# The last 64 queries of a short pair: scores of two heads in one full-size product

## The chip, the cores and the metric

The program runs on one core of one Trainium2 chip. The metric is the device time of one execution, in microseconds. Times of the kernel before: 1029.75 us median of three runs (1027.41 to 1031.17).

## The reference

One attention layer with a compressive memory, then two dense feed-forward layers. Inputs have batch 4, 8 heads, 576 positions, head size 64.

```
scores = q k^T / 8, causal;  a = softmax(scores);  local = a v
q_p = elu(q) + 1
mem = (q_p M) / (q_p z + 1e-6)            # per head, M is 64x64, z is 64
x = g * mem + (1 - g) * local             # g = sigmoid(beta), one per head
x = [2304 tokens, 512]
x = gelu-like(x w_in) w_out               # h * sigmoid(1.702 h), 512 -> 2048 -> 512
x = hswish(x w2_in) w2_out                # h * clip(h + 3, 0, 6) / 6
```

## The kernel before

The tokens are cut in six tiles of 384. A batch's first 384 queries are a tile of their own (a long segment, g = 0); its last 192 queries (a short segment, g = 1) share a tile with those of another batch. Heads go in pairs: a tile with a long segment has 4 pairs, one with two short segments has 8. Tiles 2 and 5 hold the short segments, 16 short pairs in all.

The feed-forward layers run as a stream of units (layer, tile, f), f over 16 blocks of 128 hidden features. A unit computes h (four quarters of 128 inputs, each three f32r products: L393, L395, L396), the gate (ScalarE L329, VectorE L332, ScalarE L341, GpSimd L344), and then y of the unit before (L364 to L366). h has one PSUM bank, so the next h waits until VectorE's L332 has read the last one. Tile 0 of layer 0 uses exact f32 products (L391, L362), which the trace shows as two records each.

The attention of the next tile runs beside the current tile's units, in steps that `pump` (L1023) emits between quarters. So the short pairs run beside tiles 1 and 4 of layer 0. `PG1` (L30) is the share of a tile's 128 steps over which the attention of a tile of short pairs is spread. A scheduler puts the instructions of each engine in order from modelled times; inside an engine they run strictly in that order. `chains` are generators that are stepped on as the emission goes; `need` runs one to its end.

For a short pair the steps are: `scores` (L612), which computes s for the first 128 queries of both heads (two banks), and then s4 and s5, the products of the last 64 queries of both heads with 512 and 64 keys. Head a lies in partitions 64a to 64a + 63 of q and k, so each is a product of a 64x64 piece that writes partitions 64a to 64a + 63 of the bank (L677 to L680). `soft4` (L682) takes their minimum on VectorE (L684, L685), the exponentials on ScalarE (L687, L688), the inverse on VectorE, and scales them on GpSimd (`norm`, L548). The 512-column part is turned through memory: `over` (L576) copies it as 16-bit words on ScalarE (L584) and issues a transposing DMA on SyncE (L590), and `join` (L593) copies the turned words into `pt` on VectorE (L609). The 64-column part, the diagonal block (tile `p5`, 128x64), is transposed on TensorE in `turn` (L726, bank `t4b`), and its copy goes to `t4` (L709). `mem_read` (L799) computes the memory term in bank `mem`, which VectorE scales into `mo` (L818 to L822). `weigh` (L834) sums everything in bank `o`: transposes of `mo`, products of `pt` with v, and of `t4` with v; ScalarE copies it to x (L886).

The banks of s, s4, s5, t4b, mem and o are taken from a ring of three (`bank`, L431). A run of products in a bank waits for the last reader of that bank. The loop that interleaves the pairs is at L953; the line that sets the order of a pair is L965.

Of the kernel before, what the change touches and what calls it, by code (L numbers as in the profile page):

```python
# [8 lines left out]
F32 = mybir.dt.float32  # L9
# [13 lines left out]
N0, N1 = 384, 192  # L23
# [3 lines left out]
CR = 8.5  # L27
OFF = 3
PG0 = (0.85, 0.8)
PG1 = 0.78  # L30
TB = 3
PB = 6
RB = 3
# [24 lines left out]
CROSS = 8  # L58
# [11 lines left out]


STEP = 768.0
ROUND = 352
BIG = 3.4028234e38
MZ = 132
TILES = [
# [37 lines left out]
def attention_moe_kernel(ctx: ExitStack, tc: tile.TileContext, qk0, sk0, sk1, vm0, vm1, bb, w1, w2, out):  # L114
# [305 lines left out]
    pairs = []  # L420
# [36 lines left out]
    def at_matmul(out, **args):  # L457
        on_pe[:] = [PE.matmul(out, **args).ins]  # L458
# [29 lines left out]
    def at_transpose(*args):  # L488
        on_pe[:] = [PE.transpose(*args).ins]

    def attention(ap, room, across):
# [4 lines left out]

        t4 = ap.tile([128, 2, 64], F32, tag="t4", bufs=1, name="t4")
        POOL.memset(t4, 0.0)

        def start(key, gen):  # L500
            gens[key] = chains.start(after_gates(gen, AB))
# [7 lines left out]
        def load_qk(i):  # L509

            if i >= NPAIR:
                return
            ti, si, b, g, p, _ = pairs[i]
            t = room[0].tile([128, 2 * N0], F32, tag="raw", bufs=RB if i < CROSS else RB2, name="qk")
            if g == 0:
                move(1, out=t, in_=qk0[b, p])
                qk[i] = (t[:, 0:N0], t[:, N0:2 * N0])
            else:
                for a in range(2):
                    h = slice(64 * a, 64 * a + 64)  # L520
                    move(3, out=t[h], in_=sk1[b, 2 * p + a][h])
                qk[i] = (t[:, 0:N1], t[:, N1:N1 + S])

        def load_vm(i):
            if not 0 <= i < NPAIR:
# [86 lines left out]
        def scores(i):  # L612

            ti, si, b, g, p, _ = pairs[i]
            norms[1] = ti
            q, k = qk[i]
            st = ap.tile([128, 12], F32, tag="st", name="st")
            mx, su = st[:, 0:6], st[:, 6:12]

            def product(banks, blocks):  # L620

                mm = in_a_run(free(banks[0]) + free(banks[1]))
                for o0, o1, c0 in blocks:
                    for a in range(2):
                        h = slice(64 * a, 64 * a + 64)
                        mm(
                            banks[a][:, o0:o1], lhsT=q[h, c0:c0 + 128], rhs=k[h, 0:o1 - o0], start=True, stop=True
                        )

            def soft(s, cols, dst, c):  # L630

                jobs = [(a, c0, c1, c + a * len(cols) + x) for a in range(2) for x, (c0, c1) in enumerate(cols)]
                yield
                for a, c0, c1, k in jobs:
                    masked_min(s[a][:, c0:c1], mask[:, 512 - (c1 - c0):512], BIG, mx[:, k:k + 1])
                yield
                for a, c0, c1, k in jobs:
                    d = expo(dst[a][:, c0:c1], s[a][:, c0:c1], mx[:, k:k + 1], su[:, k:k + 1])
                    if c1 == cols[-1][1]:
                        has_read(s[a], d)  # L640
                yield
                inverse(su[:, c:c + len(jobs)])
                yield
                for a, c0, c1, k in jobs:
                    norm(dst[a][:, c0:c1], su[:, k:k + 1], omg[:, 2 * p + a:2 * p + a + 1])
                if i >= CROSS:
                    yield
                    for a in range(2):
                        yield from over(i, a, dst[a], *merges0[g][c > 0])

            pp[i] = []
            if g == 0:
                parts = (((0, 128, 0), (128, 384, 128)), ((0, 384, 256),))
            else:
                parts = (((0, 512, 0),),)
            def weights(a):
                return room[0].tile([128, 512], F32, tag="p", bufs=PB2 if i >= CROSS else PB, name="p")

            t = [[None if i >= CROSS else weights(a) for _ in parts] for a in range(2)]
            pp[i] = [tuple(x) for x in t]  # L660
            c = 0
            for x, blocks in enumerate(parts):
                s = [bank("s") for _ in range(2)]
                if i >= CROSS:
                    for a in range(2):
                        t[a][x] = weights(a)
                product(s, blocks)
                start(("s", i, x), soft(s, [(o0, o1) for o0, o1, _ in blocks], [t[a][x] for a in range(2)], c))
                c += 2 * len(blocks)
                yield  # L670
            if g == 1:
                t = room[0].tile([128, 512], F32, tag="p", bufs=PB2 if i >= CROSS else PB, name="p4")
                t2 = ap.tile([128, 64], F32, tag="p5", name="p5")
                pp[i].append((t, t2))
                s, s2 = bank("s4"), bank("s5")
                mm = in_a_run(free(s) + free(s2))
                for o, c0, c1 in ((s, 0, 512), (s2[:, 0:64], 512, 576)):  # L677
                    for a in range(2):
                        h = slice(64 * a, 64 * a + 64)
                        mm(o[h], lhsT=q[h, 128:N1], rhs=k[h, c0:c1], start=True, stop=True)  # L680

                def soft4(s=s, s2=s2, t=t, t2=t2):  # L682
                    yield
                    masked_min(s, mask[:, 0:1].to_broadcast([128, 512]), BIG, mx[:, 2:3])  # L684
                    masked_min(s2[:, 0:64], mask4, mx[:, 2:3], mx[:, 3:4])  # L685
                    yield
                    has_read(s, expo(t, s, mx[:, 3:4], su[:, 2:3]))  # L687
                    has_read(s2, expo(t2, s2[:, 0:64], mx[:, 3:4], su[:, 3:4]))  # L688
                    yield
                    DVE.tensor_tensor(out=su[:, 2:3], in0=su[:, 2:3], in1=su[:, 3:4], op=ALU.add)  # L690
                    inverse(su[:, 2:3])
                    yield
                    norm(t, su[:, 2:3], omp[:, p:p + 1])
                    norm(t2, su[:, 2:3], omp[:, p:p + 1])
                    if i >= CROSS:
                        yield
                        yield from over(i, None, t, 512, [(0, 4, None)])

                start(("s", i, 2), soft4())
                yield  # L700

        def evac(i, jobs):
# [11 lines left out]
        def turn(i):  # L714
            ti, si, b, g, p, _ = pairs[i]
            if i >= CROSS:
                need(("s", i, 0), ("s", i, 1), ("s", i, 2))
                for k in (0, 1, None):
                    if k is not None:
                        head(i)  # L720
                    for n, (a, blocks, turned) in enumerate(joins[i]):
                        if a == k:
                            start(("j", i, n), join(i, a, blocks, turned))
                    if k == 1 and g == 1:
                        ps2 = bank("t4b")
                        at_transpose(ps2[0:64, 0:128], pp[i][2][1], ident)  # L726
                        start(
                            ("t", i, 0, 1),
                            evac(i, [(DVE, t4[0:64], ps2[0:64, 0:128].rearrange("p (a c) -> p a c", a=2), ps2)]),
                        )  # L730
                    yield
                if g == 0:
                    yield
# [65 lines left out]
        def mem_read(i):  # L799
# [7 lines left out]
            nb = len(rr)  # L807
            for k, r0 in enumerate(rr):
                at_matmul(a[:, k * 130:(k + 1) * 130], lhsT=e[:, r0:r0 + 128], rhs=m, start=True, stop=True)
            o = ap.tile([128, NT], F32, tag="tmp", bufs=TB, name="mo")  # L810
            w = ap.tile([128, 3, 2], F32, tag="mw", name="mw")
            mo[i] = o
# [118 lines left out]
        yield from weigh(CROSS - 1)  # L931
        across(0)
        load_qk(CROSS)
        load_qk(CROSS + 1)
        need(("x", CROSS - 1))
        yield pairs[CROSS - 1][0]
# [14 lines left out]
            yield pairs[i][0]  # L951

        for i in range(CROSS, NPAIR):  # L953
            s = scores(i)
            if i == CROSS or pairs[i - 1][5]:
                yield from chunks(s, 1)
                yield from pause(2)
                yield from chunks(s, 9)
                begun(i)
            else:  # L960
                t, w = turn(i - 1), weigh(i - 1)
                yield from chunks(s, 1)
                yield from mem_read(i - 1)
                load_qk(i + 1)
                for gen, n in ((t, 1), (s, 1), (t, 1), (s, 9), (t, 9)):  # L965
                    yield from chunks(gen, n)
                begun(i)
                yield from chunks(w, 9)
            if pairs[i][5]:
                yield from pause(WAIT[pairs[i][3]])  # L970
                yield from mem_read(i)
                load_qk(i + 2)
                yield from ended(i, turn(i), weigh(i))
# [197 lines left out]
```

## Time and profile before

| what | value |
|---|---|
| median of three runs | 1029.75 us |
| the profiled execution's own time | 1029.37 us |
| its span, first to last instruction | 1027.6 us |
| TensorE busy | 996.6 us |
| ScalarE, VectorE, GpSimd busy | 552.3, 508.6, 304.5 us |
| mean granted TensorE clock | 0.993 |

The span is the time from the first to the last instruction; 1.8 us of the execution lie outside it. Rows of an engine's timeline give start and duration of an instruction, or of several alike (x8: eight records; the duration then reaches from the first start to the last end). Starts of products that follow each other tell their cost better than the durations, since products overlap. In brackets stands the idle time ahead of an instruction and what ended it.

### The profile page before, as it was taken

The page shows a single profiled execution, that of the slowest core. Times are in us where ns is not written, and L with a number is a line of the kernel's source. Part 1 is how long each engine was busy: PE and PEld are TensorE (multiplying, and loading weights), DVE is VectorE, ACT ScalarE, POOL GpSimd, SP SyncE. Part 2 cuts the span into 40 slices and gives each one's busy share as a digit, 9 for nine tenths or more (in the row PEclk, how much of TensorE's full clock was granted, in tenths as well). Part 3 has the DMA queues.
Part 4 walks back from the last instruction along what each step waited for, and adds up shares of the span by engine and source line. Part 5 has one row for each costly group of instructions (what it writes and reads, how often), then busy time and mean ns, then how long its engine had stood idle before and what let it go on. Part 6 is the DMA issues. An engine that isn't in the chain of part 4 may idle for free.

```text
span 1027.6 us, 15875 instructions
## 1 busy us (share of the span) xinstructions
PE 996.6 (97%) x5737; PEld 883.8 (86%) x5737; DVE 508.6 (49%) x1263; ACT 552.3 (54%) x1142; POOL 304.5 (30%) x346
## 2 busy tenths in 40 slices
PE   7899999888999999999989999999999999999998
PEld 4556557677888898888869999999999999999998
DVE  5887775677655447346554887951121211212110
ACT  5877766666665466366554987963232332323322
POOL 3512003433343334243322422232222222222221
PEclk8999999999999999999999999999999999999999
DMA  4844427675453044225543773010010000100000
GB/s 168 295 184 151 157 77 195 146 184 143 113 101 101 27 101 98 55 80 122 123 108 125 296 255 134 1 32 32 1 62 1 31 32 1 47 16 1 32 1 32
DMA packets 110175, 99.15 MB, mean 96 GB/s; under 512 B 80400, under 2 KB 89616, under 8 KB 110096
## 3 DMA queue, kind: packets, MB, share of 16 engines
q1 hardware_dynamic: 110096, 98.14, 32.9%
q8 instruction: 45, 0.74, 0.3%
q14 instruction: 34, 0.28, 0.1%
HBM read 61.41 MB, written 9.44 MB: 69 GB/s over the span
## 4 chain that ended last, share of the span: by engine, by line
PE 69%; DMA 4%; DVE 3%; ACT 3%; issue 2%; POOL 1%; SPq 0%; ACTq 0%; DVEq 0%; POOLq 0%
PE h L393 11%; PE y L364 10%; PE h L395 10%; PE h L396 10%; PE y L365 10%; PE y L366 10%; DMA xp<-sp 4%; PE o L474 3%; PE s L474 2%; ACT sp L584 1%; DVE pt L609 1%; PE mem L458 1%; ACT p L540 1%; POOL p L548 1%; DVE s L535 1%
## 5 line engine op out<-in xcount | busy, mean ns | idle before, releaser
L344 POOL TENSOR_TENSOR g<-t,g 128x384 fp32r<-128x384 f32 x173 | 185.3, 1072 | 467.1 <-ACT g L341 391.9
L393 PE MATMUL h<-xs,w 128*128 128x384 f32 x704 | 242.3, 344 | 9.8 <-DVE t L332 9.7
L395 PE MATMUL h<-xs,w 128*128 128x384 f32 x704 | 236.6, 336 | 0.0
L396 PE MATMUL h<-xs,w 128*128 128x384 f32 x704 | 236.6, 336 | 0.0
L365 PE MATMUL y<-g,w 128*128 128x384 f32 x704 | 236.0, 335 | 0.0
L364 PE MATMUL y<-g,w 128*128 128x384 f32 x704 | 235.4, 335 | 0.0
L366 PE MATMUL y<-g,w 128*128 128x384 f32 x704 | 219.0, 336 | 0.0
L336 DVE SCALAR_TENSOR_TENSOR t<-t,h 128x384 f32<-128x384 f32 x96 | 53.1, 553 | 277.5 <-ACT t L334 277.4
L548 POOL TENSOR_SCALAR p<-p,st,omg 128x128 f32<-128x128 f32 (+3 forms) x128 | 93.2, 740 | 212.5 <-DVE st L544 116.7
L393 PEld LDWEIGHTS h<-xs,w 128*128 128x128 f32 x704 | 132.6, 188 | 25.8 <-DVE t L332 12.5
L334 ACT ACTIVATE t<-h,three 128x384 f32<-128x384 f32 x96 | 56.2, 585 | 170.5 <-PE h L396 167.7
L341 ACT CAST g<-t 128x384 fp32r<-128x384 f32 x176 | 91.0, 517 | 95.7 <-DVE t L336 50.2
L395 PEld LDWEIGHTS h<-xs,w 128*128 128x128 f32 x704 | 132.7, 189 | 1.5 <-issue 1.5
L396 PEld LDWEIGHTS h<-xs,w 128*128 128x128 f32 x704 | 132.6, 188 | 0.9 <-issue 0.8
L365 PEld LDWEIGHTS y<-g,w 128*128 128x128 f32 x704 | 132.2, 188 | 0.9 <-issue 0.8
L364 PEld LDWEIGHTS y<-g,w 128*128 128x128 f32 x704 | 132.2, 188 | 0.4 <-issue 0.3
L366 PEld LDWEIGHTS y<-g,w 128*128 128x128 f32 x704 | 130.2, 188 | 1.7 <-POOL g L344 1.4
L540 ACT ACTIVATE p<-s,st 128x256 f32<-128x256 f32 (+4 forms) x160 | 82.2, 522 | 62.1 <-DVE st L535 59.3
L535 DVE CUSTOM_DVE_ANT_0 s<-s,mask 128x128 f32<-128x128 f32 (+3 forms) x144 | 72.4, 528 | 30.9 <-PE s L474 30.2
L584 ACT COPY sp<-p 128x1024 uint16<-128x1024 uint16 (+1 forms) x80 | 74.8, 957 | 23.6 <-POOL p L548 17.7
L609 DVE COPY pt<-xp 128x512 uint16<-128x512 uint16 (+3 forms) x112 | 63.5, 625 | 36.0 <-DMA xp<-sp 22.2
L332 DVE SCALAR_TENSOR_TENSOR t<-t,h 128x384 f32<-128x384 f32 x80 | 43.9, 550 | 54.3 <-ACT t L329 50.5
(79 smaller groups left out, 1111.1 us busy)
## 6 DMA issues: line engine op xcount, KB each, us to landing
r<-in_w_dram SPq DMA_DIRECT2D x64, 512.0 KB, 6.1
wt<-r SPq DMA_DIRECT2D x32, 256.0 KB, 2.4
vm<-in_vm_dram SPq DMA_DIRECT2D x16, 386.0 KB, 3.4
qk<-in_qk_dram SPq DMA_DIRECT2D x16, 384.0 KB, 3.4
qk<-in_sk_dram SPq DMA_DIRECT2D x32, 192.0 KB, 3.3
x2d<-yo SPq DMA_DIRECT2D x24, 192.0 KB, 1.9
xr<-x2d SPq DMA_DIRECT2D x24, 192.0 KB, 3.1
out_dram<-yo SPq DMA_DIRECT2D x24, 192.0 KB, 1.9
```

Of the source, the lines that this page charges most:

```text
L341: gated["ACT"].append(ACT.copy(out=g[:, 0], in_=t).ins)
L344: d = {"DVE": DVE, "POOL": POOL}[e].tensor_tensor(out=g[:, 1], in0=t, in1=f32(g[:, 0]), op=ALU.subtract)
L364: PE.matmul(ys[d], lhsT=w[:, 0, o:o + 128], rhs=g[:, 0], start=(f == 0), stop=False)
L365: PE.matmul(ys[d], lhsT=w[:, 1, o:o + 128], rhs=g[:, 0], start=False, stop=False)
L366: PE.matmul(ys[d], lhsT=w[:, 0, o:o + 128], rhs=g[:, 1], start=False, stop=(f == NF - 1))
L393: PE.matmul(h, lhsT=w[:, 0, c:c + 128], rhs=x[:, 0], start=first, stop=False)
L395: PE.matmul(h, lhsT=w[:, 1, c:c + 128], rhs=x[:, 0], start=False, stop=False)
L396: PE.matmul(h, lhsT=w[:, 0, c:c + 128], rhs=x[:, 1], start=False, stop=last)
L535: DVE.tensor_tensor_reduce(out=o, in0=o, in1=m, scale=-SCALE, scalar=init, op0=ALU.add, op1=ALU.min, accum_out=out)
L540: return ACT.activation(out=dst, in_=o, func=AF.Exp, scale=-1.0, bias=m, accum_out=s)
L548: (DVE, POOL)[e[norms[0] % len(e)]].tensor_scalar(out=dst, in0=dst, scalar1=s, scalar2=w, op0=ALU.mult, op1=ALU.mult)
L584: ACT.copy(out=halves[:, 0:2 * n].rearrange("p (h c) -> p h c", h=2), in_=src[:, 0:n].bitcast(U16).rearrange("p (c h) -> p h c", h=2),)
```

## The change

Both heads' last 64 queries are put in one 128x128 tile `bd`, with the queries of head 0 in its upper left block, those of head 1 in its lower right block, and zeros elsewhere. One product of `bd` with all 128 partitions of k gives the scores of both heads, head a in partitions 64a to 64a + 63 as before. `bd` is one tile that is filled with zeros once; two DMAs per pair load its blocks, for the next short pair, after the current pair's product is emitted (`load_bd`). The diagonal block `p5` becomes one 128x128 tile whose right half stays zero; it is transposed at full size, in `mem_read`, into the free columns 384 to 511 of bank `mem`, instead of in `turn` into a bank of its own. In the loop, the second step of `scores` of a short pair comes after two steps of `turn` instead of one. `PG1` goes from .78 to .9, and an unused table is made smaller (`ROUND`).

```diff
-PG1 = 0.78
+PG1 = 0.9
-ROUND = 352
+ROUND = 32
...
         POOL.memset(t4, 0.0)
+        bd = ap.tile([128, 128], F32, tag="bd", bufs=1, name="bd")
+        POOL.memset(bd, 0.0)
+        p5 = ap.tile([128, 128], F32, tag="p5", bufs=1, name="p5")
+        POOL.memset(p5, 0.0)
...
+        def load_bd(i):
+
+            short = [pair for pair in pairs[i:] if pair[3] == 1]
+            if not short:
+                return
+            ti, si, b, g, p, _ = short[0]
+            for a in range(2):
+                h = slice(64 * a, 64 * a + 64)
+                move(3, out=bd[h, h], in_=sk1[b, 2 * p + a][h, 128:N1])
...
-                t2 = ap.tile([128, 64], F32, tag="p5", name="p5")
+                t2 = p5[:, 0:64]
...
                 for o, c0, c1 in ((s, 0, 512), (s2[:, 0:64], 512, 576)):
-                    for a in range(2):
-                        h = slice(64 * a, 64 * a + 64)
-                        mm(o[h], lhsT=q[h, 128:N1], rhs=k[h, c0:c1], start=True, stop=True)
+                    mm(o, lhsT=bd, rhs=k[:, c0:c1], start=True, stop=True)
...
                 start(("s", i, 2), soft4())
+                load_bd(i + 1)
                 yield
...
-                    if k == 1 and g == 1:
-                        ps2 = bank("t4b")
-                        at_transpose(ps2[0:64, 0:128], pp[i][2][1], ident)
-                        start(
-                            ("t", i, 0, 1),
-                            evac(i, [(DVE, t4[0:64], ps2[0:64, 0:128].rearrange("p (a c) -> p a c", a=2), ps2)]),
-                        )
...
+            if i >= CROSS and g == 1:
+                need(("s", i, 2))
+                at_transpose(a[:, 384:512], p5, ident)
+                start(("t", i, 0, 1), evac(i, [(DVE, t4[0:64], a[0:64, 384:512].rearrange("p (a c) -> p a c", a=2))]))
...
         load_qk(CROSS)
+        load_bd(CROSS)
...
-                for gen, n in ((t, 1), (s, 1), (t, 1), (s, 9), (t, 9)):
+                for gen, n in ((t, 1), (s, 1), (t, 1), (s, 9), (t, 9)) if g == 0 else ((t, 1), (t, 1), (s, 9), (t, 9)):
```

The order on TensorE, in tile 1, where the third short pair's s4 follows the second pair's mem; first before, then the change (xs and w are operands of h, g and w those of y; `s_` with the larger number is s5).

```order
L458 MATMUL mem<-vm,phi 128x130 x2
L366 MATMUL y_1400<-g,w_1334 128x384
L366 MATMUL y_1401<-g,w_1334 128x384
L366 MATMUL y_1402<-g,w_1334 128x384
L366 MATMUL y_1403<-g,w_1334 128x384
L474 MATMUL s_1660<-qk 64x512 x2
L474 MATMUL s_1661<-qk 64x64 x2
L393 MATMUL h<-xs_1291,w_1555 128x384
```

```order
L458 MATMUL mem<-vm,phi 128x130 x2
L489 MATMUL mem<-ident,p_121 128x128
L364 MATMUL y_1409<-g,w_1340 128x384
L365 MATMUL y_1409<-g,w_1340 128x384
L366 MATMUL y_1409<-g,w_1340 128x384
L474 MATMUL s_1697<-qk,bd 128x512
L474 MATMUL s_1698<-qk,bd 128x64
L393 MATMUL h<-xs_1297,w_1549 128x384
```

The group of four products has become two, and the transposition of the diagonal block stands behind mem and ahead of the next s4; before it stood some twenty products behind that s4, ahead of o.

The order on VectorE, a little later in tile 1, around the copy of the third pair's turned s4 words (`pt<-xp` with 4x64); first before, then the change (`t<-t,h` is the gate that frees the bank of h, `mw` and `mo` scale mem, `t_117<-mem` copies the transposed diagonal block, w is weight work).

```order
L609 COPY pt<-xp 128x2x4x64 x2
L543 TENSOR_SCALAR st<-st 128x2
L544 RECIPROCAL st<-st 128x2
L332 SCALAR_TENSOR_TENSOR t<-t,h 128x384
L818 TENSOR_SCALAR mw<-mem 128x4
L819 RECIPROCAL mw<-mw 128x4
L820 TENSOR_TENSOR mw<-mw,gall 128x4
L275 TENSOR_TENSOR w_1947<-wt,w_1947 128x512
L822 TENSOR_TENSOR mo<-mem,mw 128x256
```

```order
L557 TENSOR_SCALAR st<-st 128x2
L558 RECIPROCAL st<-st 128x2
L332 SCALAR_TENSOR_TENSOR t<-t,h 128x384
L623 COPY pt<-xp 128x2x4x64 x2
L722 COPY t_117<-mem 64x128
L828 TENSOR_SCALAR mw<-mem 128x4
L829 RECIPROCAL mw<-mw 128x4
L275 TENSOR_TENSOR w_1905<-wt,w_1905 128x512
L830 TENSOR_TENSOR mw<-mw,gall 128x4
L832 TENSOR_TENSOR mo<-mem,mw 128x256
```

The gate and a reciprocal have moved ahead of the copy that waits for a DMA, and the copy of the diagonal block has come in behind it.

## Rows read from the trace of the kernel before

**Rows 1.** The page, part 1: busy us (share of the span), instructions, by engine
```profile
PE 996.6 (97%) x5737; PEld 883.8 (86%) x5737; DVE 508.6 (49%) x1263; ACT 552.3 (54%) x1142; POOL 304.5 (30%) x346
```
**Rows 2.** Windows of tiles 1 and 4: length, busy PE, PEld, DVE, ACT, POOL, clock
```profile
160.00:262.00 102.00, 91.91 (x579) 74.99 (x579) 71.91 (x196) 66.76 (x140) 39.96 (x41) 0.98 0.70 165
460.00:562.00 102.00, 97.18 (x635) 81.69 (x632) 57.20 (x181) 54.45 (x117) 31.77 (x40) 0.98 0.49 111
```
**Rows 3.** Waits of TensorE, 160 to 265 us: us in total, times, longest
```profile
PE h L393 <- DVE t L332: 5.4, 4, 2.0
PE o L474 <- DVE t L709: 1.8, 1, 1.8
PE t4b L489 <- DVE mo L822: 1.4, 1, 1.4
PE o L474 <- ACT p L540: 0.9, 1, 0.9
```
**Rows 4.** Waits of TensorE, 440 to 565 us
```profile
PE o L474 <- ACT p L540: 2.9, 1, 2.9
```
**Rows 5.** Timeline of TensorE around an s4 group: start, duration, instruction
```profile
541.24 0.34 PE L366 MATMUL y<-g,w 128*128 128x384 f32 x1
541.51 1.19 PE L474 MATMUL s<-qk 64*64 64x512 f32 x8
542.63 0.44 PE L393 MATMUL h<-xs,w 128*128 128x384 f32 x1
542.91 0.34 PE L395 MATMUL h<-xs,w 128*128 128x384 f32 x1
543.09 0.34 PE L396 MATMUL h<-xs,w 128*128 128x384 f32 x1
```
**Rows 6.** Exact f32 products of tile 0: group (busy, mean ns), then timeline
```profile
L391 PE MATMUL h<-x,r 128*128 128x384 f32 x128 | 44.8, 493 | 1.4 <-DVE g L332 1.2 <-ACT pt L707 0.2
...
139.50 2.85 PE L391 MATMUL h<-x,r 128*128 128x384 f32 x8 [0.31 <-DVE g L332]
```
**Rows 7.** Timeline of TensorE around mem and the next s4
```profile
194.29 0.61 PE L458 MATMUL mem<-vm,phi 128*128 128x130 f32 x4
...
194.91 0.33 PE L366 MATMUL y<-g,w 128*128 128x384 f32 x1
195.18 1.19 PE L474 MATMUL s<-qk 64*64 64x512 f32 x8
198.41 0.45 PE L393 MATMUL h<-xs,w 128*128 128x384 f32 x1 [2.04 <-DVE t L332]
```
**Rows 8.** Timeline of TensorE around a transposition of the diagonal block
```profile
185.49 0.27 PE L489 MATMUL t4b<-ident,p 128*64 128x128 f32 x1
185.52 0.42 PE L365 MATMUL y<-g,w 128*128 128x384 f32 x1
185.78 0.34 PE L366 MATMUL y<-g,w 128*128 128x384 f32 x1
```
**Rows 9.** Timeline of VectorE from one copy of turned s4 words to the next
```profile
196.84 0.79 DVE L609 COPY pt<-xp 128x512 uint16<-128x512 uint16 x2 [2.94 <-DMA xp<-sp]
...
197.80 0.55 DVE L332 SCALAR_TENSOR_TENSOR t<-t,h 128x384 f32<-128x384 f32 x1
...
200.40 0.69 DVE L535 CUSTOM_DVE_ANT_0 s<-s,mask 128x512 f32<-128x512 f32 x1
...
212.34 0.79 DVE L609 COPY pt<-xp 128x512 uint16<-128x512 uint16 x2 [2.64 <-DMA xp<-sp]
```
**Rows 10.** Timeline of GpSimd: scaling of both parts of an s4
```profile
220.97 3.13 POOL L548 TENSOR_SCALAR p<-p,st,omp 128x512 f32<-128x512 f32 x2
```
**Rows 11.** Timeline of TensorE: the s4 that this scaling belongs to
```profile
211.00 1.19 PE L474 MATMUL s<-qk 64*64 64x512 f32 x8
```
**Rows 12.** Timeline of SyncE: transposing DMAs of the pair of rows 7, two loads
```profile
200.92 2.66 SPq L590 DMA_TRANSPOSE xp<-sp  x2
203.74 1.14 SPq L156 DMA_DIRECT2D qk<-in_sk_dram  x2
```

More of the change, by code (lines that the diff above doesn't have):

```diff
@@ L953, in attention @@
         for i in range(CROSS, NPAIR):
+            g = pairs[i][3]
             s = scores(i)
```

## The prediction

> **What bounds the kernel now.** I read the busy shares first, then the waits of TensorE by stretch, then its timeline around the instructions that change. TensorE is busy 996.6 us, 97% of the span, and every other engine but its own weight loader at most 54% [rows 1], so a change counts only if it shortens TensorE's own stream or one of its stops. The changed work lies in two stretches in which the short pairs run beside a tile of layer 0: tile 1 (160 to 262 us) and tile 4 (460 to 562 us). There TensorE stands still for 102.0 - 91.9 = 10.1 and 102.0 - 97.2 = 4.8 us [rows 2]. The waits name what ended each stop [rows 3, 4]: a gate on VectorE that frees the bank of h, the exponentials on ScalarE that free the bank of the s4 product, and the copy of the transposed diagonal block.
>
> **The product (16 times).** Before, one group computes 512 and 64 columns for the two heads in 64x64 pieces, 8 records. One f32r product of 384 columns follows another after .18 us; the group starts .27 after its predecessor, takes 1.12 to the next start, and the product behind it needs .28 [rows 5]. So a group costs 1.12 + .09 + .10 = 1.31 us, and 16 cost 21.0. After, one product of the whole array does the same columns in 2 + 2 records. Exact full-size products of 384 columns are .337 us apart (eight take 2.85 and a single one .493, so (2.85 - .493) / 7 [rows 6]), .88 ns a column, so two records of 512 take .90. For the 64 columns the bounds are two records at .88 ns a column (.11) and two that take as long as the 130 columns of mem: four of those cost .62 - .18 = .44, .11 each [rows 7], so .22. I take .16. The same mem rows go from f32r to exact full-size products and back with no extra start time, so I add none. The new group costs 1.01 to 1.12, taken 1.06: .25 saved each, **4.0 us in all, bounds 3.0 to 4.8**.
>
> The Trainium skill, "TensorEngine Tiling (Array Packing)", Theoretical Speedup, gives up to 2x to a dimension of at most 64; read against this change, giving up the 64-row pieces would double the streaming and cost some 16 x 1.0 us. The rows speak otherwise here: the 8 records before need 1.12 us for two heads side by side, and one full-size product holds both heads at once, so it streams the columns once, as before. By the rule the time would be some 16 us longer, by the rows 4.0 shorter; I give the rule no chance of its own beyond the slow rival.
>
> **The transposition.** The 64-column one before costs .29 - .18 = .11 us between products [rows 8]; the full-size one streams 128 columns like a record of mem, .11 [rows 7]. I count 0, bounds -.3 and +.3 for 16. The Trainium skill, same page, Gotcha 2: Feature Incompatibilities, says that column tiling excludes the transpose mode for FP32; by it the full-size form should gain more than that, and the .11 before leaves it no room.
>
> **Stops that go.** A short pair took seven banks of three in turn: two s, mem, s4, s5, t4b, o. So o took the bank that s4 had just filled, and waited for its exponential, .9 us in tile 1 and 2.9 in tile 4 [rows 3, 4]; t4b took mem's and waited 1.4 for VectorE; and once o waited 1.8 for the copy out of t4b [rows 3]. With t4b inside mem's bank there are six: o takes mem's bank, which it needs emptied anyway, and the block is copied before the scaling of mem. These four stops, 7.0 us, lose their cause. What is late next is o's other inputs, the turned words of s4 and mem's scaled rows.
>
> **What holds part of it.** VectorE copies the turned words of a pair's s4 when their DMA lands, and what stands behind that copy waits with it. For the third pair the copy waited 2.94 us, and behind it the gate that frees h, which stopped TensorE for 2.04 [rows 7, 9]. In the changed order the gate stands ahead of the copy, so this stop and its like (rows 3: 5.4 us in four) move. But the minimum of the next s4 still stands behind the copy: 196.84 to 200.40, and from there to the next such copy 212.34, a cycle of 15.5 us [rows 9]. The gate leaves it (.55 [rows 9]); a reciprocal that leaves and the copy of the block that enters about cancel: some 15. TensorE's work per pair is the distance of two s4, 211.00 - 195.18 = 15.8, less the stop of 2.04: 13.8, after 13.5 [rows 7, 11]. So where the cycle rules, I take three pairs of tile 1, 15 - 13.5 = 1.5 us each stay as a stop, now in front of o: 4.5 us, and their .8 us of saved product time is swallowed too.
>
> **A wait that comes.** The transposition of the diagonal block now stands behind mem, ahead of the next s4. It needs the block scaled on GpSimd; all of TensorE's queue, the h and y products included, stands behind it. The longest case: s4 at 211.00, scaled at 220.97 + 3.13 = 224.10, 13.1 us later [rows 10, 11]; the third pair's s4 has its next mem some 12 us behind it by the changed order (36 to 40 f32r products at .18, one o, one s, one s4). I take 2.0 us in all for these waits, bounds 0 and 8.
>
> **Loads, fills, pace.** 32 loads of 64x64 enter SyncE's queue; one issue takes .57 us (1.14 for two [rows 12]), so 1.14 per pair. Each waits for the s4 that read the tile last, and the transposing DMAs of the next pair stand behind it; the fourth pair's came at 200.92, 5.7 us after its s4 at 195.18 [rows 7, 12], so the load hides in idle queue time. If each delay reached TensorE: 15 x 1.1 = 17 us, the far end. The two fills on GpSimd run before its first work: 0, at most the 3.1 us that two scalings took [rows 10]. The slower pace (.9 for .78) moves, in the order, only the last pair of a tile: its o now comes with little between it and the last quarter of the next tile's h. I charge .5 at each of two borders, 1.0 in all; bounds 0 and 2.0 each, the longest stop of an h.
>
> **The sum.** Tile 1: stops 10.1 before; after, 4.5 of the cycle, 2.0 of the block and some 1.0 of gates that nothing here touches, 7.5: -2.6. Tile 4, with no weight work on VectorE: 4.8 before, the 2.9 goes, some .3 comes: -2.6. Products -4.0, of which .8 is swallowed: -3.2. Borders +1.0. Together -7.4 us. The profiled execution took 1029.4 (span 1027.6), the median of the runs is 1029.75; 1029.4 - 7.4 gives **1022.0 us**, .8% under the median.
>
> **Rivals.** A: only the products get shorter, and every stop that goes comes back before o or s4, since the cycle through the DMA sets the pace in all pairs. For it: the 15.5 us cycle. Against: tile 4 has hardly a stop besides o's 2.9. Time: 1029.4 - 4.0 = 1025.4. B, slower: the early transposition blocks TensorE. It decides if the block is ready some 2 us later after its s4 than before, for VectorE and GpSimd work no less; then the 12 us of room are short in about half of 15 pairs by 1 us and in the like of the 13.1 case by 3, some 10 us with the stops of rows 3 and 4 kept: 1029.4 - 4.0 + 10 = 1035.4; at half that lateness 1030.4. For it: 13.1 in one pair of tile 1. Against: elsewhere in these stretches GpSimd idles for microseconds ahead of that scaling. C: the cycle was only a result of the stops, and nearly all 14.9 us of them shrink to 5: 1029.4 - 4.0 - 9.9 = 1015.5. That the block-diagonal tile isn't loaded in time, so that s4 waits for its DMA, is part of B: a load has the 13.5 us of a pair's work to land in.
>
> **Chances.** Forecast .55 (own range 1017 to 1024.6), A .26, B .11, C .08. The range that holds 8 in 10 is 1015 to 1030, from C's end to half of B. A measurement of this kernel tells about .5% from no change, so faster means under 1024.6: the forecast's .52, C's .08, and a little of A's, .05, .65 in all; slower means over 1034.9, or .07 of B and a bit of unknown, .08; the rest, .27, within.
>
> **What would show it.** The new s4 group should stand .18 behind its predecessor, last 1.0 to 1.1 us, and leave no longer second start behind it. The waits of o for an exponential and all of t4b should be gone. o should wait for the words' copy or mem's rows in tile 1, by 1 to 2 us in some pairs; the new transposition for GpSimd in one or two. I am wrong if the stops of the two stretches sum to over 13 us, if a DMA of the block-diagonal tile ends a wait of s4, or if full-size exact products of 512 columns come over .5 us a record.

## The result and the profile after

The changed kernel took 1016.74 us (median of four runs, 1014.47 to 1017.99) against 1030.46 of the kernel before on the same chip: ratio .9867, 95% interval .9836 to .9899. That is 13.7 us less, where 7.4 were forecast. It lies inside the range of 1015 to 1030 us, .3 below the forecast's own range (1017 to 1024.6), and nearest to rival C (1015.5), which had a chance of .08.

The head of the page of the changed kernel, to be read against [rows 1]:

```profile
span 1012.6 us, 15781 instructions
PE 988.6 (98%) x5673; PEld 884.6 (87%) x5673; DVE 513.0 (51%) x1263; ACT 551.4 (54%) x1142; POOL 307.4 (30%) x348
```

Its two stretches by windows (us, then busy time of TensorE, its loader, VectorE, ScalarE, GpSimd, then granted clock), against [rows 2]:

```profile
160.00:262.00 102.00, 94.81 (x587) 80.11 (x586) 76.72 (x204) 69.69 (x147) 41.70 (x43) 1.00 0.72 172
460.00:562.00 102.00, 101.39 (x644) 91.07 (x643) 67.81 (x184) 63.49 (x131) 37.71 (x40) 1.00 0.58 140
```

TensorE stands still for 7.2 us in tile 1 (10.1 before) and .6 in tile 4 (4.8 before). Its waits in the first stretch, against [rows 3] (total, times, longest):

```profile
PE s L474 <- ACT p L554: 2.2, 5, 0.8
PE h L393 <- DVE t L332: 2.0, 2, 1.1
PE o L474 <- DVE mo L832: 1.9, 1, 1.9
PE o L474 <- DVE pt L623: 0.8, 1, 0.8
PE mem L489 <- POOL p L562: 0.2, 1, 0.2
```

and in the second, against [rows 4]:

```profile
PE o L474 <- DVE mo L832: 0.6, 1, 0.6
```

No stop of o for an exponential is left, and t4b is gone. No stop is ended by a DMA of `bd`; those loads land 2.2 us after issue (median). The new group, against [rows 5] (start, duration):

```profile
477.12 0.33 PE L365 MATMUL y<-g,w 128*128 128x384 f32 x1
477.30 1.19 PE L474 MATMUL s<-qk,bd 128*128 128x512 f32 x4
478.29 0.42 PE L366 MATMUL y<-g,w 128*128 128x384 f32 x1
478.55 0.34 PE L364 MATMUL y<-g,w 128*128 128x384 f32 x1
```

It starts .18 behind its predecessor and takes .99 to the next start; the start after that comes .26 later, not the usual .18. So it costs .99 + .08 = 1.07 us, against 1.06 forecast and 1.31 before.

**Where the time went.** I split the span of each profiled run in three. Stops are the span less TensorE's busy time on the page. Clock is the sum of (1 - granted clock) x 4 us over windows of 4 us, up to 1000 us. The rest is busy time less that loss.

| | span | stops | clock | rest |
|---|---|---|---|---|
| before | 1027.6 | 31.0 | 6.8 | 989.8 |
| after | 1012.6 | 24.0 | 1.7 | 986.9 |
| difference | -15.0 | -7.0 | -5.1 | -2.9 |

The profiled runs differ by a little more than the medians. The changed kernel's was its fastest, with a mean granted clock of .998; the other three had .994 to .997, so part of the 5.1 us of clock belongs to this one run. Of these 5.1 us, 1.7 fall in the first 100 us, which the change hardly touches. The others stand behind two stops of the kernel before, one of 1.7 us in tile 1 (an h that starts at 213.89) and the one of 2.9 us that [rows 4] show. Around the latter:

```profile
526.00:532.00 6.00, 3.14 (x19) 1.91 (x17) 4.01 (x16) 3.46 (x7) 1.53 (x2) 0.98 0.26 60
532.00:538.00 6.00, 6.00 (x34) 3.98 (x35) 2.29 (x6) 1.91 (x5) 2.12 (x3) 0.74 0.35 95
```

After the stop the clock is .74 over 6 us, 1.6 us lost on top of the stop itself. The changed kernel has no such window between 100 and 1000 us.

### The profile page after: what moved, and what is told of

Read it like the earlier page. It is cut to its first block, busy times and chain, and to the rows that moved or that the text cites. A ratio compares the mean times of both kernels' runs of the same rounds, so it can differ in the third digit from the quotient of the medians.

```text
span 1012.6 us, 15781 instructions
## 1 busy us (share of the span) xinstructions
PE 988.6 (98%) x5673; PEld 884.6 (87%) x5673; DVE 513.0 (51%) x1263; ACT 551.4 (54%) x1142; POOL 307.4 (30%) x348
## 4 chain that ended last, share of the span: by engine, by line
PE 78%; DVE 7%; ACT 6%; DMA 5%; issue 3%; SPq 1%; POOL 1%; POOLq 0%; ACTq 0%; DVEq 0%
PE h L393 11%; PE y L366 11%; PE h L395 11%; PE h L396 11%; PE y L364 11%; PE y L365 11%; DMA xp<-sp 3%; PE o L474 3%; PE h L391 3%; PE y L362 3%; PE s L474 3%; ACT p L554 2%; DVE s L549 1%; ACT sp L598 1%; PE mem L458 1%
## 5 line engine op out<-in xcount | busy, mean ns | idle before, releaser
L623 DVE COPY pt<-xp 128x512 uint16<-128x512 uint16 (+3 forms) x112 | 68.6, 667 | 21.7 <-DMA xp<-sp 18.4
```

## The experiments

Each was timed in five rounds beside the kernel before, whose median was 1029.4 to 1029.8 us in the three sets. The forecast gave the gain to three things: the product, the shorter ring of banks, and the stops that go with it. The rivals were that it comes from the pace, and that the parts don't add.

**The parts, one at a time.** The kernel before with the product and its loads alone:

```
+                load_bd(i + 1)
...
-                    for a in range(2):
-                        h = slice(64 * a, 64 * a + 64)
-                        mm(o[h], lhsT=q[h, 128:N1], rhs=k[h, c0:c1], start=True, stop=True)
+                    mm(o, lhsT=bd, rhs=k[:, c0:c1], start=True, stop=True)
```

> The kernel before with the block-diagonal product and its loads alone; the transposition, its bank, the loop and the pace (.78) stay. My theory (products 4 us, the rest from stops of TensorE that go with the smaller ring of banks): 4 us faster than before, ratio .996, with the waits of o for an exponential and of t4b still there, since the ring still has seven banks a pair. Rival (the saved product time is swallowed where the copy of the turned words sets the pace): 2 us or less, .998. In either case the new group takes .99 us to the next start instead of 1.12 and starts .18 behind its predecessor instead of .27.

Measured: 1037.62 us, ratio 1.0076 [1.0054, 1.0099]. The shorter group alone makes the kernel slower. Its waits over the whole run (stops 35.4 us, before 31.0):

```profile
PE h L393 <- DVE t L332: 9.6, 9, 1.9
PE s L474 <- ACT p L552: 9.1, 7, 2.3
```

The same two in the kernel before:

```profile
PE h L393 <- DVE t L332: 9.7, 8, 2.0
PE s L474 <- ACT p L540: 2.3, 2, 1.8
```

So the waits that came are those of s for an exponential that frees its bank. Six of the seven are stops of s4, 6.8 us in all, against one of .5 us before.

The changed kernel without the product (64x64 pieces and no `bd`, the rest as changed):

> The changed kernel with the 64x64 products of before (no block-diagonal tile, no loads of it); early full-size transposition in mem's bank, loop and pace (.9) as changed. My theory: 4 us slower than the changed kernel, ratio to before .9905, stops of TensorE as in the changed kernel (some 20 us). Rival (the product is what makes the rest fit): stops come back to 27 us and the ratio is .995 or more.

Measured: 1023.35 us, ratio .9938 [.9919, .9957]. So in the changed kernel the same product is worth 6.6 us (1023.35 - 1016.74; 7.3 by the two ratios, each known to some 3 us).

The changed kernel at the old pace:

```
-PG1 = 0.9
+PG1 = 0.78
```

> The changed kernel with the pace of before, .78. The order on VectorE then has the gate of h behind the copy of the turned words again in five of seven pairs of tile 1, ahead of it in one; the ring of six banks stays. My forecast's account (pace costs 1 us at the borders, stops go with the ring of banks): 1 us faster to 2 slower than the changed kernel, ratio .986 to .989. Rival (the pace puts the gate ahead of the copy, and that is where the stops go): 4 to 7 us slower than the changed kernel, ratio .991 to .994, with waits of h for the gate of 2 us each back in tile 1.

Measured: 1032.76 us, ratio 1.0025 [1.0011, 1.0040]: there the pace is worth 16 us. What comes back (4.6, 4.4 and 2.5 us in the changed kernel):

```profile
PE s L474 <- ACT p L554: 11.5, 12, 2.1
PE h L393 <- DVE t L332: 6.3, 8, 2.1
PE o L474 <- DVE mo L832: 5.4, 5, 2.1
```

The kernel before at the new pace (`PG1 = 0.9`, nothing else):

> The kernel before with the pace .9 alone. On VectorE the gate then stands ahead of the copy in most pairs, while s4, the transposition and the ring of seven banks are as before. My forecast's account: no faster than before (ratio .998 to 1.002), since the stops of o and t4b belong to the ring. Rival (pace): 4 to 7 us faster, ratio .993 to .996.

Measured: 1023.25 us, ratio .9937 [.9916, .9958]. The pace, which I had charged with +1.0 us, brings 6.5 by itself, and the early transposition in six banks adds nothing to it (1023.35 with both). The parts don't add: the product is worth +7.8 or -6.6 us, by what stands beside it.

**The product at the new pace, with the late transposition.** The kernel before with both:

```
-PG1 = 0.78
+PG1 = 0.9
...
+                    mm(o, lhsT=bd, rhs=k[:, c0:c1], start=True, stop=True)
```

> The kernel before with the full-size block-diagonal product, its loads and the pace .9; the block is still transposed late, in a bank of its own, in 64 columns, and the loop order is that of before. Theory (pace and product are the whole gain; the early transposition and the shorter ring are worth nothing, as the pair of runs with the 64x64 products said): 1016 to 1018.5 us, ratio .987 to .989. Rival (the product pays only once o no longer shares a bank with s4, as my prediction's ring had it): 1021 to 1025 us, ratio .991 to .995, with waits of o for the exponential of s4 of 3 us or more and of the late transposition for VectorE over 1 us.

Measured: 1033.54 us, ratio 1.0034 [1.0014, 1.0054]. Both expectations are missed, on the slow side: at this pace the product costs 10.3 us with the late transposition (1033.54 - 1023.25), so it needs something of the early one. Against the changed kernel the profiled run is 19.2 us longer: 12.0 of stops (8.2 of them in tile 4, 455 to 580 us, and 3.3 in tile 1, 160 to 275 us), 5.1 of clock, 2.1 of the rest. In tile 1, o waits for an exponential in five stops, 3.3 us in all, the wait that my ring of seven has; the changed kernel has none there. Tile 4 shows another kind, in a few rows of VectorE, one of ScalarE and one of TensorE:

```profile
508.38 1.77 DVE L621 COPY pt<-xp 128x1024 uint16<-128x1024 uint16 x2 [1.07 <-PE o L474]
513.74 0.80 DVE L621 COPY pt<-xp 128x512 uint16<-128x512 uint16 x2 [3.59 <-DMA xp<-sp]
514.43 0.69 DVE L547 CUSTOM_DVE_ANT_0 s<-s,mask 128x512 f32<-128x512 f32 x1
```

```profile
515.22 0.69 ACT L552 ACTIVATE p<-s,st 128x512 f32<-128x512 f32 x1 [5.86 <-DVE st L547]
```

```profile
516.72 1.47 PE L474 MATMUL s<-qk,bd 128*128 128x512 f32 x4 [2.00 <-ACT p L552]
```

The minimum of the next pair's s (514.43) stands on VectorE behind both kinds of copies of turned words: one waits for o to read the last `pt`, the other for its DMA. s itself starts at 508.92 on TensorE and takes 1.1 us, so the minimum is 4.4 us late. ScalarE stands still for 5.86 before the exponential, and s4 stops for 2.00 until the exponential has read its bank. Two such stops of s4 make 3.5 of the 8.8 us that TensorE stands still in tile 4; in the pair before this one the minimum is 1.6 us late, and s4 has no stop. In the changed kernel the copy of s4's words stands behind both minima in tile 4, so that its own waits for the DMA (1.80 us at 500.72) don't delay them.

**Is it the ring of banks?** The late transposition, written into the free columns of mem's bank, so that a pair takes six banks:

```
-                        ps2 = bank("t4b")
-                        at_transpose(ps2[0:64, 0:128], pp[i][2][1], ident)
+                        ps2 = ma.pop(i)
+                        at_transpose(ps2[0:64, 384:512], pp[i][2][1], ident)
```

> The kernel with product and pace .9 but the late transposition (1033.54 us), with one thing changed: the late, 64-column transposition writes into the free columns of the bank of mem instead of a bank of its own, so that a short pair takes six banks. Theory of the ring (what the changed kernel has over that one is that o takes the bank of mem, not that of s4): 1016 to 1021 us, ratio .987 to .992. Rival (it is the order on VectorE: in tile 4 the copies of the turned words stand ahead of the minimum of the next s in both kernels, and wait there for o and for the DMA): 1029 to 1034 us, ratio 1.0 to 1.004, with stops of TensorE in 455 to 580 us of 6 us or more.

Measured: 1033.32 us, ratio 1.0041 [1.0026, 1.0057]: no faster than with seven banks. But two things cancel in it. Stops fall from 36.0 to 31.2 us, while the rest of TensorE's time grows from 989.0 to 996.3. In five pairs the products of s, two heads side by side in four records, are pulled apart:

```profile
202.66 1.12 PE L474 MATMUL s<-qk 64*128 64x512 f32 x2
203.71 0.45 PE L393 MATMUL h<-xs,w 128*128 128x384 f32 x1
...
205.24 1.12 PE L474 MATMUL s<-qk 64*128 64x512 f32 x2
206.29 0.33 PE L474 MATMUL o<-t,vm 128*64 128x64 f32 x2
```

Each half takes 1.05 us to the next start; the four records together take 1.06 elsewhere. Five pairs lose some 5.2 us so.

The changed kernel with the block in a bank of its own, transposed as early as there, so that a pair takes seven:

```
-                at_transpose(a[:, 384:512], p5, ident)
+                ps2 = bank("t4b")
+                at_transpose(ps2[:, 0:128], p5, ident)
```

> The changed kernel, but the block is transposed, as early as there, into a bank of its own, so that a short pair takes seven banks again and o takes the one that s4 filled. Theory of the ring (my prediction): o waits for the exponential of s4 again, 4 to 7 us in all, 1021 to 1024 us, ratio .991 to .994. Rival (the ring is worth nothing): 1016 to 1018.5 us, ratio .987 to .989. A third outcome: the order of VectorE shifts (in this kernel the gate that frees the bank of h stands behind the copy of the turned words in most pairs of tile 1, as at the pace .78); if that order is what the pace buys, h and s wait as at .78: 1026 us or more, ratio over .996, without waits of o for the exponential.

Measured: 1036.62 us, ratio 1.0065 [1.0041, 1.0089], 20 us over the changed kernel. It is nearest to the third outcome, with another cause than I wrote there for part of it. With the transposition between mem and s4, s5 takes the bank of mem, and the whole run of s4 and s5 waits until VectorE has scaled mem:

```profile
257.93 0.42 DVE L833 TENSOR_TENSOR mo<-mem,mw 128x256 f32<-128x256 f32 x1
```

```profile
258.46 2.37 PE L474 MATMUL s<-qk,bd 128*128 128x512 f32 x4 [3.02 <-issue]
```

The profile names no releaser there; by time it is that scaling, which ends .11 us before, and in three more stops of this kind it ends .11 to .12 before too. These four stops sum to 6.2 us. The transposition itself now waits for GpSimd, 4.0 us in two stops (3.3 in one of tile 4). So the ring does matter for an early transposition, not by the wait of o for s4 that I had named.

**Is it the order on VectorE?** The copies of turned words are held back until the minima of the next pair's s are issued; nothing else is edited:

```
-                with tc.issue_after(gated["DVE"][-1]):
+                with tc.issue_after(gated["DVE"][-1]), tc.issue_after(least[0]):
                     d = DVE.tensor_copy(out=out.bitcast(U16)...
```

First on the kernel with the product at .78 (1037.62 us):

> The kernel before with the product alone at the pace .78 (1037.62 us), with the same hold on the copies: here it moves the order in tile 1 as well as in tile 4 (minimum, minimum, copy, copy in all pairs). Theory of VectorE's order: what the product lost there comes back, and its shorter groups show: 1026 to 1031 us, ratio .996 to 1.001. Rival (the ring of seven, or the pace, is what the product cannot stand): 1035 to 1039 us, ratio over 1.005.

Measured: 1023.83 us, ratio .9953 [.9941, .9965]: 13.8 us less than without the hold, more than expected, and 5.6 under the kernel before. Without the hold, s4's words (here `128x512`) had come ahead of a minimum in one pair of tile 1 and in three of tile 4. VectorE and TensorE of the product alone, in that pair of tile 1:

```profile
208.32 1.38 DVE L621 COPY pt<-xp 128x1024 uint16<-128x1024 uint16 x2
...
210.18 0.79 DVE L621 COPY pt<-xp 128x512 uint16<-128x512 uint16 x2
210.86 0.70 DVE L547 CUSTOM_DVE_ANT_0 s<-s,mask 128x512 f32<-128x512 f32 x1
```

```profile
205.54 1.13 PE L474 MATMUL s<-qk 64*128 64x512 f32 x4
213.16 2.25 PE L474 MATMUL s<-qk,bd 128*128 128x512 f32 x4 [2.17 <-ACT p L552]
```

s is done by 206.7, its minimum starts 4.2 us later, and s4 stops for 2.17 us until the exponential has read the bank. With the hold:

```profile
205.25 0.70 DVE L547 CUSTOM_DVE_ANT_0 s<-s,mask 128x512 f32<-128x512 f32 x1 [1.50 <-PE s L474]
205.86 0.73 DVE L547 CUSTOM_DVE_ANT_0 s<-s,mask 128x512 f32<-128x512 f32 x1
206.51 1.39 DVE L621 COPY pt<-xp 128x1024 uint16<-128x1024 uint16 x2
```

```profile
203.98 1.13 PE L474 MATMUL s<-qk 64*128 64x512 f32 x4
208.89 1.19 PE L474 MATMUL s<-qk,bd 128*128 128x512 f32 x4
```

The minimum starts as soon as s is there (VectorE waits for it), and s4 has no stop. In 455 to 580 us TensorE stands still for 2.3 us (125.0 - 122.7) against 7.7 without the hold. In tile 1 (160 to 275 us) nothing is gained in sum, 13.3 us against 12.8: other stops take the place of those that went, the longest a late transposition that waits 2.4 us for VectorE. The profiled runs differ by 10.1 us (that of the product alone was its fastest): 5.2 of stops, 3.4 of clock, 1.5 of the rest. The hold without the product wasn't run, so the 5.6 us are not the product's worth.

Then the same hold on the kernel with product, pace .9 and late transposition. It moves the copies of s4's words in tile 4 alone; the other copies (`128x1024`) go behind the minima in tile 1 too, which the expectation leaves out:

> The kernel with product, pace .9 and the late transposition in seven banks (1033.54 us), with the copies of the turned words held back on VectorE until the minima of the next pair's s are issued. This moves the order in tile 4 alone (copy, minimum, copy, minimum becomes minimum, minimum, copy, copy); tile 1 stays. Theory of VectorE's order: the stops of 455 to 580 us fall from 8.7 to 3 us or less, the clock drop there goes, 1022 to 1027 us, ratio .992 to .998. Rival (the ring of seven): o and s still wait for exponentials, 1031 to 1035 us, ratio over 1.001.

Measured: 1029.85 us, ratio 1.0003 [.9991, 1.0016]: 3.7 us less than without it. That lies between the two expectations. In 455 to 580 us the waits sum to 6.0 us, not 3, and the clock drop there stays (1.7 us lost); s no longer waits there for an exponential, but h, t4b and o wait for VectorE and GpSimd. In tile 1 TensorE stands still for 12.3 us, 11.8 without the hold. Order is part of it there, not all.

**The loop and the pace.** The changed kernel with the loop of before:

```
-                for gen, n in ((t, 1), (s, 1), (t, 1), (s, 9), (t, 9)) if g == 0 else ((t, 1), (t, 1), (s, 9), (t, 9)):
+                for gen, n in ((t, 1), (s, 1), (t, 1), (s, 9), (t, 9)):
```

> The changed kernel with the loop of the short pairs as before: one s after the first step of the pair, then the rest. Theory (the loop order is off the path): 1016 to 1018 us, ratio .987 to .988. Rival (it is part of why the stops are small): 1020 to 1024 us, ratio .990 to .994, with s waiting for the exponential over 7 us in all where the changed kernel has 4.6.

Measured: 1015.96 us, ratio .9865 [.9840, .9890]. The loop's order is worth nothing.

The changed kernel at `PG1 = 1.0` and `PG1 = 0.95`:

> The changed kernel with the pace at 1.0 for .9. Theory (what the pace buys is that VectorE's gate stands ahead of the copy of the turned words: it does so in every pair of both tiles here): 1013 to 1017 us, ratio .983 to .988, with the waits of h for the gate under 4 us. Rival (a pace of .9 is a best point between two costs: slower attention leaves its last pairs to the border, where nothing stands between their steps): 1020 to 1026 us, ratio .990 to .997, with stops of over 5 us more at 262 to 275 and 562 to 575 us.

> The changed kernel at the pace .95; .78 gave 1032.76 us, .9 gave 1016.74, 1.0 gave 1020.02. If the time follows the pace smoothly with a best point between: 1015 to 1018 us, ratio .986 to .988. If single places in the order decide: anything from 1013 to 1024 us, with a stop of over 2 us at a place where neither .9 nor 1.0 has one.

Measured: 1020.02 us, ratio .9908 [.9884, .9931], and 1019.96 us, ratio .9919 [.9905, .9933]. So .9 is the best of the four tried, but the time doesn't follow the pace smoothly: each of these two has a long stop of its own. At 1.0 an h waits 4.4 us in tile 1. At .95 tile 1 is as good as at .9, and a single h behind tile 4 waits 4.00 us:

```profile
541.61 0.44 PE L393 MATMUL h<-xs,w 128*128 128x384 f32 x1 [4.00 <-DVE t L332]
```

No version measured beats the changed kernel by more than the runs can tell.

## Why the prediction was right, and where it was not

Sign and range were right; the sum was short by 6.3 us, and one of its causes was wrong. That the total still fell in the range is in part luck. In the profiled runs, where 7.6 us are missing (15.0 - 7.4), 5.1 are clock, which the sum left out, 1.6 the stops of tile 4, 1.0 the borders and .3 the stops of tile 1; the products gave .3 less.

- **Product.** A group takes 1.07 us, forecast 1.06, so 16 save 3.8 us; no start time was lost on entry. Two slips cancel in it: the records take .99, under my bounds of 1.01 to 1.12, and a longer second start (.26) stands behind them that I said would not be there. The rest of TensorE's time fell by 2.9. The Trainium skill's rule that I weighed there ("TensorEngine Tiling (Array Packing)", Theoretical Speedup), as I read it against this change, would by my estimate have cost some 16 us; the rows after rule that reading out here.
- **Transposition.** As forecast, nothing on TensorE (the next two starts come .03 and .26 us behind it, as in [rows 8]), and two stops before it for GpSimd, .5 us in all for 2.0 charged.
- **Stops.** Tile 1 was forecast at 7.5 us and has 7.2, tile 4 at 2.2 and has .6. They are of the kinds forecast (o for mem's rows and for the words' copy) and of one not forecast: s for an exponential, 2.2 us in five. That tile 1 comes out so near is luck: 4.5 in front of o, 2.0 for the block and 1.0 for gates were forecast; 2.7, .2 and 2.0 are there, and the 2.2.
- **Their cause: the step that failed.** I gave the four stops, 7.0 us, to the ring that goes from seven banks to six. The pace alone takes 6.5 us from the kernel before with the ring of seven, and ring and early transposition on top of it nothing. With the product at the pace .9 they pay only together: with neither, with six banks alone and with the early transposition alone its kernels take 1033.5, 1033.3 and 1036.6 us, with both 1016.7. Each of the two in the middle has a cost of its own (5.2 us of products pulled apart, 6.2 us of s4 behind mem), so the ring by itself was not isolated. What the runs show in its place, in part, is the order on VectorE: holding the copies of turned words behind the minima was worth 13.8 us at the pace .78 and 3.7 at .9. Whether the place of the gate matters likewise was not tested. The scheduler sets the order from modelled times, so each edit moves it.
- **Borders.** I charged the slower pace with +1.0 us. TensorE's busy time from 262 to 300 us is 36.66 us before and 36.65 after, and from 562 to 600 us 38.00 in both: nothing. The pace was the edit that I had priced with the wrong sign.
- **Clock.** Not in my sum: between 100 and 1000 us the loss of clock behind stops is 3.4 us before and 0 in the profiled run after.
- **Rival C** was nearest. Its number fits better than its account: it took stops of 5 us in the two stretches, where 7.8 are left, and no clock. It said that the cycle on VectorE was a result of the stops, and the cycle in tile 1 is now 15.0, 13.7, 15.4, 12.8 and 12.6 us between copies, where TensorE's own work asks for 13.5. So it is clearly longer than that work in two pairs, where my forecast had three at 15.

What stays open: why the late transposition costs the product 17 us at pace .9 (the hold gives back 3.7), and which of the small moves on VectorE the pace of .9 owes its gain to. A kernel with the order of the changed one but the ring of seven wasn't tried, nor the kernel before with the hold alone.

## What to carry to other kernels

When a scheduler sets the order from modelled times, an edit on one engine moves the order on the others; price an edit of the pace or of a product by the rows where the order changes on the waiting engine, not by its own duration. A wait-bound instruction (a copy behind a DMA) should stand behind the short one that starts the next chain (the minimum that feeds the exponential): that order was worth 13.8 us in one kernel here and 3.7 in another, the shorter products by themselves some 4. Parts of such a change are not to be judged alone: the product cost 7.8 us by itself and brought 6.6 with the rest.

## What the runs showed of the hardware

A long stop of TensorE can cost more than its length. In the kernel with early transposition and seven banks, around the stop of 3.02 us shown above:

```profile
254.00:258.00 4.00, 1.44 (x11) 1.20 (x9) 2.04 (x11) 1.29 (x6) 0.88 (x2) 0.93 0.35 66
258.00:262.00 4.00, 3.54 (x12) 2.04 (x14) 2.21 (x7) 2.09 (x3) 0.64 (x1) 0.50 0.46 70
```

The clock is .50 (1.2 of 2.4 GHz) right after it, and the s4 group takes 2.37 us there for 1.19 at full clock. In the 14 profiles, the loss of clock between 100 and 1000 us was always near a multiple of 1.7 us: 0 after the change, 3.4 before, 10.2 in this kernel. I had not counted that. Length alone doesn't tell which stop brings it: in the kernel before, the stop of 2.04 us of [rows 7] is followed by full clock, the one of 1.7 us at 213.89 by .57 over 214 to 218 us.
